# A fused attention and feed-forward kernel: first loads made plain, the first chunk's mask put on TensorE, x transposed by DMA, feed-forward in smaller pieces, and a planner with priorities

## The chip, the cores and the metric

The kernel runs on one core of one Trainium2 chip. The metric is device time in microseconds (us) of one execution; lower is better. For the kernel before there are three timed runs and one profiled execution. A busy time or a duration below is from that profiled execution, whose times count from the first instruction.

## The reference

Block-sparse attention, and then a feed-forward layer on its output. Four batches, 8 heads, 768 positions, head size 64. The mask works on blocks of 32 positions: neighbours, the first and the last block, and three sampled blocks for each block of queries.

```python
scores = q @ k.T / sqrt(64)
mask = |block_i - block_j| <= 1, or block 0 / 23 on either side, or block_j in sampled_blocks[block_i]
attn = softmax(where(mask, scores, -1e9))
x = (attn @ v) as 3072 tokens x 512            # 4*768 tokens, 8 heads * 64
xn = x / sqrt(mean(x*x) + 1e-6) * rms_g
g = xn @ w_gate                                # 512 x 1536
val = xn @ w_val                               # 512 x 1536
out = (g * sigmoid(g) * val) @ w_out           # 1536 x 512, float32
```

## The kernel before

Work is cut into 12 chunks of 256 queries, three to a batch. A chunk has 12 tiles: 4 pairs of heads (`pr`) by 3 pairs of key blocks (`j2`). For a tile, `scores` (L448) runs four matmuls of 256 columns into a two-bank PSUM tile `s_` (two buffers, token `s`). Each contracts over 64 rows, the two heads of a pair sitting in rows 0 to 63 and 64 to 127. `exp_` (L459, ACT) turns `s_` into the bf16 tile `pt`, `mask_` (L466, DVE) multiplies `pt` by the 0/1 tile `Mk`, and `av` (L479) multiplies it with `va`, which carries a column of ones, into `o_` (one buffer, token `o`). After a pair's three tiles `o_norm` (L491, L494, DVE) divides by the sum of the row and writes `x`. After four pairs `square` (L502, ACT) and `rstd` (L508, L510, POOL) give the RMS factor, `scale_x` (L515, DVE) applies it, `x_transposes` (L525, PE) turns the chunk over into PSUM, and `x_copy` (L532, DVE) writes `xn`, scaled by `gcol`.

The feed-forward of chunk u has six steps f. In each, `product` (L608) makes 8 matmuls for the gate (`gp`) and 8 for the value (`vp`), in one of three one-bank buffers (token `f`). ACT takes tanh (`th`, L618), DVE makes `uu` (L622) and `hp` (L632). `ff_y` (L642) then makes two halves of 12 matmuls of 512 columns; ACT copies each out (`yo`, L649), and the SP queue stores it (L651).

The opening loads batch 0 by casting DMAs on the POOL queue (`load_q` L198, `load_k` L202, `vraw` L258), transposes q and k on PE (`tq`, L328) with copies on DVE and ACT (L334), and builds the masks with GpSimd selects (`Bm`, `Kind`), matmuls (`qm` L367, `mp` L375) and copies (L389, L381). Weights come by four half loads and `wo` (L299, L302). Later batches are loaded piece by piece (L208, L412) and q and k are transposed by DMA on the SP queue (L355).

The order of nearly all this is set by `Plan`, which runs when the kernel is built. Each task has engines with assumed durations, dependencies and tokens. At each step the task with the least key is put on its engine: the start time, then a priority. A gate adds `HOLD` to the time of a scores task that would run too far ahead of the feed-forward (`LEAD` tiles), or whose pair of `s` buffers isn't both free soon. `SOLO` says up to which tile scores tasks hold one tile; from there on they hold two. With `SOLO = 144` all of the 144 tiles are single tasks, and two of them stand side by side only where the planner happens to put them so. Engines then run their lists strictly in that order.

Of the kernel before, what the change touches and what calls it, by code (L numbers as in the profile page):

```python
# [15 lines left out]
HOLD = 1.0  # L16


class Plan:
# [10 lines left out]
    def add(self, name, engines, fn, deps=(), prio=5, acq=(), rel=(), mode=None, lat=0.12,  # L30
            dma=None, after=0.0, gate=None, work=0.0):
        self.seq += 1
        assert name not in self.tasks, name
        self.tasks[name] = dict(
            name=name, engines=engines, fn=fn, deps=list(deps), prio=prio, acq=list(acq),
            rel=list(rel), mode=mode, lat=lat, dma=dma, after=after, gate=gate, work=work,
            seq=self.seq)
# [5 lines left out]
    def run(self, log=None):  # L43
        self.free = free = {e: 0.0 for e in ("PE", "ACT", "DVE", "POOL", "SP")}
        busy = {e: 0.0 for e in free}
# [3 lines left out]
        dma_free = 17.0  # L49
# [15 lines left out]
        while left:  # L65
            best = None
            for name in ready:
# [17 lines left out]
                for e, dur in t["engines"].items():  # L85
# [4 lines left out]
                    key = (round(eager + wait, 3), t["prio"], start + dur, t["seq"])  # L90
# [36 lines left out]
def kernel(  # L127
# [32 lines left out]
    ppool = ctx.enter_context(tc.tile_pool(name="ppool", bufs=3))  # L160
# [14 lines left out]

    plan = Plan()
    for name, n in (("s", 2), ("o", 1), ("f", 3), ("pt", 3), ("x1", 2), ("x2", 3), ("xn", 3),
                    ("hp", 2), ("th", 3), ("uu", 3), ("yo", 3), ("qk", 2), ("raw", 1)):
        plan.pool(name, n)

    samp_i = const.tile([32, 2 * NRND], I32, name="samp_i")
# [4 lines left out]
    gcol = const.tile([P, KC], FP32, name="gcol")  # L186
    nc.sync.dma_start(out=gcol, in_=moe_rms_g.rearrange("(c p) -> p c", p=P))
# [16 lines left out]
    def load_c(b, i, c):  # L204
# [7 lines left out]
    load_q(0, 2, 0, 2)  # L212
    load_k(0, 2)

# [4 lines left out]
    nhalf = const.tile([P, 2], FP32, name="nhalf")  # L219
    nc.vector.memset(nhalf, -0.5)  # L220
    Bm = const.tile([32, 32], BF16, name="Bm")
    nc.vector.memset(Bm, 1.0)
    Kind = const.tile([32, NC, P], BF16, name="Kind")
    nc.vector.memset(Kind, 1.0)
    Kindf = Kind.rearrange("b c p -> b (c p)")
# [3 lines left out]
    jb = const.tile([32, 32], I32, name="jb")  # L229
    nc.gpsimd.iota(jb, pattern=[[1, 32]], base=0, channel_multiplier=0)  # L230
    nc.gpsimd.affine_select(
        out=Bm, in_=Bm, compare_op=ALU.is_ge, fill=0.0,
        base=1, pattern=[[-1, 32]], channel_multiplier=1)
    nc.gpsimd.affine_select(
        out=Bm, in_=Bm, compare_op=ALU.is_ge, fill=0.0,
        base=1, pattern=[[1, 32]], channel_multiplier=-1)
    for base in (0, -(NB - 1)):
        nc.gpsimd.affine_select(
            out=Bm, in_=Bm, compare_op=ALU.not_equal, fill=1.0,
            base=base, pattern=[[0, 32]], channel_multiplier=1)  # L240
    nc.gpsimd.affine_select(
        out=Kind, in_=Kind, compare_op=ALU.is_ge, fill=0.0,
        base=0, pattern=[[1, NC], [NC, P]], channel_multiplier=-32)
    nc.gpsimd.affine_select(
        out=Kind, in_=Kind, compare_op=ALU.is_ge, fill=0.0,
        base=31, pattern=[[-1, NC], [-NC, P]], channel_multiplier=32)

# [3 lines left out]

    load_q(2, 8, 0, 2)
    load_k(2, 4)
    load_k(4, 8)
    va = [const.tile([P, H, NC, D + 2], BF16, name=f"va{i}") for i in range(2)]
    vraw = raw.tile([P, H, NC * D], BF16, name="vraw")
    for lo in (0, 4):
        nc.gpsimd.dma_start(out=vraw[:, lo:lo + 4, :], in_=vv[0, :, lo:lo + 4, :])  # L258
# [8 lines left out]
    jbf = const.tile([32, 32], FP32, name="jbf")  # L267
# [3 lines left out]
    nc.vector.memset(Bm[:, 0:1], 1.0)  # L271
    nc.vector.memset(Bm[:, NB - 1:NB], 1.0)
    for r in range(NRND):
        nc.vector.scalar_tensor_tensor(
            out=Bm[0:NB, 0:NB], in0=jbf[0:NB, 0:NB], scalar=samp_f[0:NB, r:r + 1],
            in1=Bm[0:NB, 0:NB], op0=ALU.is_equal, op1=ALU.max)

# [9 lines left out]
    def pe(cols, n=1):  # L287
# [3 lines left out]
    K_AT = {0: 5.5, 1: 9.0, 2: 12.0, 3: 12.0}  # L291
    V_AT = (15.0, 17.6)
    plan.add("qrest", {"POOL": 0.8}, lambda e: load_q(0, 8, 2, 6), deps=[">wg0", ">wv0"], dma=4.2,
             prio=5, after=9.0)
    for half in range(2):
        for nm, dst, src in (("wg", wg, wgv), ("wv", wv, wvv)):
# [42 lines left out]
    for pr, i, c0, c1 in TP:  # L339
# [4 lines left out]
                 deps=["qrest"] if c0 else [])  # L344
# [15 lines left out]
    Qvis = const.tile([32, S], BF16, name="Qvis")  # L360
    Mk = const.tile([P, NIC, NC, CQ], BF16, name="Mk")
    mps = {}

    def mask_query(ic):
        cols = slice(ic * CQ, (ic + 1) * CQ)
        qm = fbank("qm")
        nc.tensor.matmul(  # L367
            out=qm[0:32, 0:CQ], lhsT=Bm[0:NB, :], rhs=Kindf[0:NB, cols], start=True, stop=True)
        mps["q", ic] = qm

    def mask_tile(ic, j2):
        mp = fbank("mp")
        cols = slice(ic * CQ, (ic + 1) * CQ)
        for j in range(2):
            nc.tensor.matmul(  # L375
                out=mp[:, j * CQ:(j + 1) * CQ], lhsT=Kind[0:NB, 2 * j2 + j, :],
                rhs=Qvis[0:NB, cols], start=True, stop=True)
        mps[ic, j2] = mp

    def mask_copy(e, ic, j2):  # L380
        (nc.scalar.copy if e == "ACT" else nc.vector.tensor_copy)(  # L381
            out=Mk[:, ic, 2 * j2:2 * j2 + 2, :].rearrange("p j q -> p (j q)"),
            in_=mps.pop((ic, j2)))

    for ic in range(NIC):
        at = 8.0 if ic == 0 else 14.0 + 4 * ic
        plan.add(f"mq{ic}", {"PE": 0.3}, lambda e, ic=ic: mask_query(ic), acq=["f"], mode="m",
                 prio=1 + ic, after=at, lat=0.2)
        plan.add(f"mqc{ic}", {"DVE": dve1(256)}, lambda e, ic=ic: nc.vector.tensor_copy(  # L389
            out=Qvis[:, ic * CQ:(ic + 1) * CQ], in_=mps.pop(("q", ic))[0:32, 0:CQ]),  # L390
            deps=[f"mq{ic}"], rel=["f"], prio=0)
        for j2 in range(NC // 2):
            plan.add(f"mt{ic}_{j2}", {"PE": 0.3}, lambda e, ic=ic, j2=j2: mask_tile(ic, j2),
                     deps=[f"mqc{ic}"], acq=["f"], mode="m", prio=1 + ic, lat=0.2)
            plan.add(f"mk{ic}_{j2}", {"DVE": dve1(512), "ACT": act(512)},
                     lambda e, ic=ic, j2=j2: mask_copy(e, ic, j2),
                     deps=[f"mt{ic}_{j2}"], rel=["f"], prio=0)
# [3 lines left out]
    for b in range(1, B):  # L401
# [9 lines left out]
        for c in range(NC):  # L411
            plan.add(f"v{b}_{c}", {"POOL": 0.9}, lambda e, b=b, c=c: nc.gpsimd.dma_start(  # L412
# [15 lines left out]

    st, pts, ots, x1s, x2s, mss = {}, {}, {}, {}, {}, {}
# [5 lines left out]
    LEAD = 28  # L435
    SPEED = 1.0
    SOLO = 144
# [3 lines left out]
    def scores(t):  # L441
# [4 lines left out]
        for jj in range(2):  # L446
            for e in range(2):
                nc.tensor.matmul(  # L448
                    out=s_[:, e, jj * CQ:(jj + 1) * CQ],
                    lhsT=x[64 * e:64 * e + 64, 1, 2 * j2 + jj, pr, :],  # L450
                    rhs=x[64 * e:64 * e + 64, 0, 2 * ic:2 * ic + 2, pr, :],
                    start=True, stop=True)
# [33 lines left out]
    def o_norm(ch, pr):  # L486
# [6 lines left out]
        for qt in range(2):  # L493
            nc.vector.tensor_tensor(  # L494
                out=x1s[ch][:, qt, 2 * pr:2 * pr + 2, :], in0=o4[:, qt, :, 0:D],
                in1=rz[:, 2 * qt:2 * qt + 2].unsqueeze(2).to_broadcast([P, 2, D]), op=ALU.mult)
# [32 lines left out]
    def x_copy(ch):  # L529
        xns[ch] = xpool.tile([P, KC, CQ], BF16, name="xn", tag="xn", bufs=3)  # L530
        for c in range(KC):
            nc.vector.tensor_scalar(  # L532
                out=xns[ch][:, c, :], in0=xts[ch][:, c, :],
                scalar1=gcol[:, c:c + 1], scalar2=None, op0=ALU.mult)

    SPT = {}
# [3 lines left out]
    for run in runs:  # L540
# [8 lines left out]
        if prev:  # L549
            deps.add(">" + prev)  # L550
        prev = f"s{i}"
        plan.add(f"s{i}", {"PE": pe(256, 2 * len(run))}, lambda e, run=run: [scores(t) for t in run],
                 deps=sorted(deps), acq=["s"] * len(run), mode="s", prio=2, lat=0.2,
                 gate=lambda i=i: (i % 2 or not PAIRED or plan.soon("s", 2)) and i <= LEAD + SPEED * len(TILES) * plan.done_work / FTOT)
# [5 lines left out]
    for ch, pr, j2 in TILES:  # L560
# [4 lines left out]
        if prev:  # L565
# [3 lines left out]
        plan.add(f"m{n}", {"DVE": dve2(1024)}, lambda e, t=(ch, pr, j2): mask_(t),  # L569
                 deps=[f"x{n}", f"mk{ic}_{j2}"], prio=3)  # L570
        deps = [f"m{n}"]
        if b == 0:
            deps.append(f"va0_{pr // 2}")
        else:
            deps += [f"v{b}_{c}" for c in (2 * j2, 2 * j2 + 1)]
        if j2:
            deps.append(f">av{ch}_{pr}_{j2 - 1}")
        plan.add(f"av{n}", {"PE": 8 * 0.0292}, lambda e, t=(ch, pr, j2): av(t),
                 deps=deps, acq=["o"] if j2 == 0 else [], rel=["pt"] if j2 == NJ - 1 else [],
                 mode="f", prio=3, lat=0.2)  # L580
    for ch in range(NCH):
        for pr in range(NP):
            plan.add(f"on{ch}_{pr}", {"DVE": 0.2 + 2 * dve1(128)},
                     lambda e, ch=ch, pr=pr: o_norm(ch, pr), deps=[f"av{ch}_{pr}_{NJ - 1}"],
                     acq=["x1"] if pr == 0 else [], rel=["o"], prio=1)
# [5 lines left out]
        for qt in range(2):  # L591
            plan.add(f"sc{ch}_{qt}", {"DVE": dve2(512)}, lambda e, ch=ch, qt=qt: scale_x(ch, qt),
                     deps=[f"rs{ch}"] + ([f">sc{ch}_0"] if qt else []), acq=["x2"],
                     rel=["x1"] if qt else [], prio=0)
        plan.add(f"xt{ch}", {"PE": 0.46}, lambda e, ch=ch: x_transposes(ch),
                 deps=[f"sc{ch}_0", f"sc{ch}_1"], acq=["f", "xn"], rel=["x2", "x2"], mode="f", prio=0, lat=0.2)
        plan.add(f"xc{ch}", {"DVE": 4 * dve2(256)}, lambda e, ch=ch: x_copy(ch),
# [5 lines left out]
    def product(w, u, fp, name):  # L603
        pp = fbank(name)
# [31 lines left out]
    YP = 3  # L636
# [90 lines left out]
```

## Time and profile before

| what | value |
|---|---|
| median of 3 runs | 326.82 us (326.37 to 327.65) |
| profiled execution | 325.57 us, its span 323.9 us |
| mean granted TensorE clock | 0.979 |
| busy share of the span | PE 94%, DVE 77%, ACT 66%, POOL 24% |
| first feed-forward matmul | at 37.46 us |
| one chunk where it has settled | 24.26 us |

The profiled execution is 1.25 us under the median of the runs, and its span 1.67 us under its own time. A span that is worked out for the changed kernel therefore becomes a time by adding 1.67 us, and a median by 1.25 us more. A busy PE is not a PE at its peak, since ends of matmuls are modelled; starts are what durations are taken from where instructions follow one another.

### The profile page before, as it was taken

The numbers are of one execution on the slowest core, as the hardware profiler recorded it, in microseconds if no ns is written. First come the engines' busy times: TensorE is split into PE (matmuls) and PEld (weight loads), VectorE is DVE, ScalarE is ACT, GpSimd is POOL, SyncE is SP. The second block draws the span as 40 slices with busy tenths as digits, with TensorE's granted clock in tenths as the row PEclk, the third lists the DMA queues.
The fourth block names the chain that finished last, engine by engine and source line by source line (L and its number), as shares of the span: only waits on it lengthen the run. The fifth ranks groups of instructions, "written<-read, shape, count | busy, mean of one in ns | idle before, by whom it ended". The sixth has DMA issues, their size and how long they took to land.

```text
span 323.9 us, 8037 instructions
## 1 busy us (share of the span) xinstructions
PE 304.8 (94%) x3368; PEld 204.2 (63%) x3389; DVE 249.4 (77%) x533; ACT 214.3 (66%) x296; POOL 76.5 (24%) x107
## 2 busy tenths in 40 slices
PE   6875999997999999999999999999999999999995
PEld 2353677575657756757747757757757757768682
DVE  4596799787958979977977968968968968957280
ACT  1684489879579676676676776776776776643221
POOL 8841747105942119070010010010010010010000
PEclk9995699999999999999999999999999999999999
DMA  3999999973999709999000000000000000010101
GB/s 35 171 210 206 208 167 134 157 151 26 143 153 196 72 2 155 94 148 192 4 32 34 2 32 34 2 32 35 2 34 33 2 34 32 2 35 32 47 21 65
DMA packets 87016, 25.68 MB, mean 79 GB/s; under 512 B 77252, under 2 KB 83908, under 8 KB 86980
## 3 DMA queue, kind: packets, MB, share of 16 engines
q0 software_dynamic: 64048, 14.16, 53.4%
q1 hardware_dynamic: 22932, 11.02, 16.0%
q8 instruction: 26, 0.43, 0.6%
q14 instruction: 10, 0.08, 0.1%
HBM read 28.31 MB, written 6.29 MB: 107 GB/s over the span
## 4 chain that ended last, share of the span: by engine, by line
PE 82%; DVE 9%; ACT 3%; POOL 2%; issue 2%; DMA 1%; POOLq 0%; DVEq 0%; ACTq 0%
PE yp L642 20%; PE gp L608 18%; PE vp L608 18%; DVE pt L466 3%; PE xT L525 1%; PE tq L328 1%; ACT junk L502 1%; DMA kb<-in_k_dram 1%; DVE uu L622 1%; ACT pt L459 1%; DVE hp L632 1%; DVE x L494 1%; PE mp L375 1%; DVE x L515 1%; POOL rs L510 1%
## 5 line engine op out<-in xcount | busy, mean ns | idle before, releaser
L466 DVE TENSOR_TENSOR pt<-pt,Mk 128x1024 bf16<-128x1024 bf16 x144 | 98.5, 698 | 10.1 <-ACT pt L459 8.9
L608 PE MATMUL vp<-xn,wv 128*128 128x256 bf16 x576 | 74.8, 273 | 0.2 <-DVE hp L632 0.2
L608 PE MATMUL gp<-xn,wg 128*128 128x256 bf16 x576 | 74.7, 273 | 0.1
L642 PE MATMUL yp<-wo,hp 128*128 128x512 bf16 x267 | 68.4, 380 | 1.3 <-DVE hp L632 0.2
L618 ACT ACTIVATE th<-gp 128x512 bf16<-128x512 f32 x72 | 43.1, 599 | 34.4 <-PE gp L608 34.4
L608 PEld LDWEIGHTS <-wv 128*128 128x128 bf16 x576 | 53.5, 98 | 11.9 <-issue 4.9
L622 DVE SCALAR_TENSOR_TENSOR uu<-th,gp 128x512 bf16<-128x512 bf16 x72 | 49.1, 683 | 15.0 <-ACT th L618 14.6
L608 PEld LDWEIGHTS <-wg 128*128 128x128 bf16 x576 | 52.5, 98 | 9.2 <-issue 2.3
L479 PEld LDWEIGHTS <-pt 128*128 128x128 bf16 x1152 | 45.8, 99 | 18.4 <-issue 7.8
L632 DVE TENSOR_TENSOR hp<-uu,vp 128x512 bf16<-128x512 bf16 x72 | 49.2, 684 | 6.3 <-PE vp L608 2.6
L508 POOL TENSOR_SCALAR rs<-ms 128x2 f32<-128x2 f32 x12 | 2.8, 233 | 189.4 <-ACT junk L502 189.4
L642 PEld LDWEIGHTS <-hp 128*128 128x128 bf16 x288 | 24.6, 97 | 26.2 <-issue 4.6
L448 PEld LDWEIGHTS <-qkT 64*128 64x128 bf16 x576 | 19.2, 95 | 30.5 <-issue 27.3
L649 ACT ACTIVATE yo<-yp 128x512 f32<-128x512 f32 x24 | 14.3, 596 | 17.4 <-PE yp L642 17.3
L515 DVE TENSOR_SCALAR x<-x,rs 128x512 bf16<-128x512 f32 x24 | 11.9, 536 | 15.6 <-POOL rs L510 15.6
L412 POOL DMA_DIRECT2D va<-in_v_dram x18 | 16.1, 948 | 7.9 <-PE o__2376 L479 7.4
L208 POOL DMA_DIRECT2D qb<-in_q_dram x18 | 15.8, 922 | 6.4 <-DMA wo<-in_moe_w_out_dram 5.6
L208 POOL DMA_DIRECT2D kb<-in_k_dram x18 | 16.3, 924 | 3.0 <-DMA qkT<-kb 3.0
L502 ACT ACTIVATE junk<-x 128x512 bf16<-128x512 f32 x24 | 14.8, 625 | 1.8 <-DVE x L494 1.8
L532 DVE TENSOR_SCALAR xn<-xT,gcol 128x256 bf16<-128x256 bf16 x48 | 13.5, 343 | 1.6 <-PE xT L525 1.5
L525 PE MATMUL xT<-ident,x 128*128 128x128 bf16 x96 | 7.9, 226 | 5.5 <-DVE x L515 3.6
L525 PEld LDWEIGHTS <-x 128*128 128x128 bf16 x96 | 6.4, 100 | 8.2 <-DVE x L515 4.2
(479 smaller groups left out, 364.1 us busy)
## 6 DMA issues: line engine op xcount, KB each, us to landing
out_dram<-yo SPq DMA_DIRECT2D x24, 256.0 KB, 2.0
kb<-in_k_dram POOLq DMA_DIRECT2D x18, 128.0 KB, 5.6
qb<-in_q_dram POOLq DMA_DIRECT2D x18, 128.0 KB, 6.6
va<-in_v_dram POOLq DMA_DIRECT2D x18, 128.0 KB, 7.4
wg<-in_moe_w_gate_dram POOLq DMA_DIRECT2D x2, 768.0 KB, 16.2
wv<-in_moe_w_val_dram POOLq DMA_DIRECT2D x2, 768.0 KB, 19.2
wo<-in_moe_w_out_dram POOLq DMA_DIRECT2D x1, 1536.0 KB, 29.6
vraw<-in_v_dram POOLq DMA_DIRECT2D x2, 384.0 KB, 8.3
```

Of the source, the lines that this page charges most:

```text
L208: nc.gpsimd.dma_start(out=flat[:, c * DM:(c + 1) * DM].rearrange("p (h d) -> p h d", h=H), in_=src[b, :, :, c * D:(c + 1) * D])
L412: plan.add(f"v{b}_{c}", {"POOL": 0.9}, lambda e, b=b, c=c: nc.gpsimd.dma_start(out=va[b % 2][:, :, c, 0:D], in_=vv4[b, :, :, c, :]), deps= ...
L448: nc.tensor.matmul(out=s_[:, e, jj * CQ:(jj + 1) * CQ], lhsT=x[64 * e:64 * e + 64, 1, 2 * j2 + jj, pr, :], rhs=x[64 * e:64 * e + 64, 0, 2 ...
L466: nc.vector.tensor_tensor(out=pv, in0=pv, in1=m.unsqueeze(1).to_broadcast([P, 2, 2 * CQ]), op=ALU.mult)
L479: nc.tensor.matmul(out=o_[:, qt, e, 0:D + 1], lhsT=pt[:, j2, e, jj * CQ + qt * P:jj * CQ + (qt + 1) * P], rhs=va[(ch // NIC) % 2][:, 2 * p ...
L502: nc.scalar.activation(out=junk, in_=x1s[ch][:, qt].rearrange("p h d -> p (h d)"), func=AF.Square, scale=float(DM) ** -0.5, accum_out=mss[ ...
L525: nc.tensor.transpose(out=xts[ch][:, c, qt * P:(qt + 1) * P], in_=x2s[ch, qt][:, c * P:(c + 1) * P], identity=ident)
L608: nc.tensor.matmul(out=pp[:, i * CQ:(i + 1) * CQ], lhsT=w[:, c, f * P:(f + 1) * P], rhs=xns[u][:, c, :], start=(c == 0), stop=(c == KC - 1))
L618: nc.scalar.activation(out=ths[u, fp], in_=gst[u, fp], func=AF.Tanh, scale=0.5)
L622: nc.vector.scalar_tensor_tensor(out=uus[u, fp], in0=ths.pop((u, fp)), scalar=1.0, in1=gst.pop((u, fp)), op0=ALU.add, op1=ALU.mult)
L632: nc.vector.tensor_tensor(out=hps[u][:, 2 * fp:2 * fp + 2, :].rearrange("p f t -> p (f t)"), in0=uus.pop((u, fp)), in1=gst.pop((u, fp, "v" ...
L642: nc.tensor.matmul(out=yst[u, t], lhsT=hps[u][:, f, t * P:(t + 1) * P], rhs=wo[:, f, :], start=(f == 0), stop=(f == NF - 1))
```

## The change

- Constants of the planner: `HOLD` 41.978, `LEAD` 29, the priority (from a table `PRIO`) times `SOFT` is added to the key's time, and engines start at times other than zero.
- `SOLO = 24`: from tile 24 on, scores tasks hold two tiles.
- Opening: the first heads of q and k are loaded plain in float32 by the ACT and SP queues (`qf`, `kf`) and cast on ACT; `v` of batch 0 is loaded plain by SP and cast by POOL. POOL's selects for the mask are replaced by one iota and DVE operations. The rest of q is loaded ahead of the weights.
- Chunk 0 (`PEMASK`) has no `mask_`: each of its scores matmuls is followed by one that adds a large negative number where the mask is 0 (`KindG`, `NegQ`). The `Mk` tiles come later.
- `av` of chunk 0 uses an `f` bank for each second pair; `pt` has four buffers and not three.
- `o_norm` is one operation for the two query halves. `scale_x` multiplies by the RMS factor and `gB` (rms_g broadcast) at once.
- Chunks 1 to 10: x is transposed by two DMAs on the SP queue straight into `xn`. Chunks 0 and 11 keep PE and one copy.
- Feed-forward: each product is cut into two tasks of four matmuls, `ff_y` into six parts, each of which waits only for the `hp` it reads. The last steps use `s` buffers. The last output is copied and stored in two halves.

```diff
-HOLD = 1.0
+HOLD = 41.978
+SOFT = 0.0051
+LEAD = 29
+PRIO = {'av': 4, 'e': 6, 'g': -5, 'h': -6, 'm': 16, 'mk': -2, 'mt': 4, 'on': -2, 'rs': 21, ...}
-                    key = (round(eager + wait, 3), t["prio"], start + dur, t["seq"])
+                    key = (round(eager + wait + SOFT * t["prio"], 3), start + dur, t["seq"])
...
+    nc.sync.dma_start(out=kf, in_=kv[0, :, 0:2, :])
+    nc.scalar.dma_start(out=qf, in_=qv[0, :, 0:2, 0:2 * D])
...
+        nc.gpsimd.memset(vraw[:, lo:lo + 4, 0:1], 0.0)
+        nc.sync.dma_start(out=vraw[:, lo:lo + 4, :], in_=vv[0, :, lo:lo + 4, :])
...
-    SOLO = 144
+    SOLO = 24
...
                 nc.tensor.matmul(
                     out=s_[:, e, jj * CQ:(jj + 1) * CQ],
...
-                    start=True, stop=True)
+                    start=True, stop=ch not in PEMASK)
+                if ch in PEMASK:
+                    nc.tensor.matmul(
+                        out=s_[:, e, jj * CQ:(jj + 1) * CQ], lhsT=KindG[rows, 2 * j2 + jj, :],
+                        rhs=NegQ[rows, ic * CQ:(ic + 1) * CQ], start=False, stop=True)
...
-        nc.vector.tensor_scalar(
+        nc.vector.scalar_tensor_tensor(
             out=x2s[ch, qt], in0=x1s[ch][:, qt].rearrange("p h d -> p (h d)"),
-            scalar1=mss[ch][:, qt:qt + 1], scalar2=None, op0=ALU.mult)
+            scalar=mss[ch][:, qt:qt + 1], in1=gB, op0=ALU.mult, op1=ALU.mult)
...
+    def x_dma(ch, qt):
+        if qt == 0:
+            xns[ch] = xpool.tile([P, KC, CQ], BF16, name="xn", tag="xn", bufs=3)
+        nc.sync.dma_start_transpose(
+            out=xns[ch][:, :, qt * P:(qt + 1) * P], in_=x2s[ch, qt])
+
+    XDMA = range(1, NCH - 1)
...
+                 gate=lambda i=i: (i % 2 or not PAIRED or i < SOLO or plan.soon("s", 2)) and i <= plan.lead + ...)
...
-    YP = 3
+    YP = 6
...
+        if (u, t) == (NCH - 1, 1):
+            lo, hi = slice(0, DM // 2), slice(DM // 2, DM)
```

What the lists look like is seen at three places. The first is ACT's list in the settled part, where an `ACTIVATE pt` is the exp of one scores tile (the number in `s__` names the PSUM tile), `th` the tanh of a feed-forward step. Before:

```order
L459 ACTIVATE pt<-s__4574 128x1024
L618 ACTIVATE th<-gp 128x512
L459 ACTIVATE pt<-s__4609 128x1024
L618 ACTIVATE th<-gp 128x512
L459 ACTIVATE pt<-s__4651 128x1024
L618 ACTIVATE th<-gp 128x512
```

After:

```order
L525 ACTIVATE pt<-s__3785 128x1024
L525 ACTIVATE pt<-s__3790 128x1024
L715 ACTIVATE th<-gp 128x512 x2
L525 ACTIVATE pt<-s__3873 128x1024
L525 ACTIVATE pt<-s__3878 128x1024
L715 ACTIVATE th<-gp 128x512
```

Scores tiles, which had stood one by one between the feed-forward steps, stand in twos. Counted over PE's whole list, the scores matmuls stand in 116 unbroken runs before and in 79 after; from the first gate matmul on, in 108 and in 66. Of tiles 12 to 143, 23 runs of two and 86 of one have become 61 of two and 10 of one.

The second is DVE's list in chunk 0, from the copies of the transposed q and k to the first division. Before:

```order
L334 COPY qkT<-tq 128x6x128
L466 TENSOR_TENSOR pt<-pt,Mk 128x1024 x3
L491 RECIPROCAL rz<-o__313 128x4
L494 TENSOR_TENSOR x_340<-o__313,rz 128x128 x2
L466 TENSOR_TENSOR pt<-pt,Mk 128x1024
L389 CAST Qvis<-qm 32x256
L491 RECIPROCAL rz<-o__358 128x4
```

After:

```order
L298 COPY Bm<-Bm 24x24
L365 COPY qkT<-tq 128x2x128
L365 COPY qkT<-tq 128x6x128
L365 COPY qkT<-tq 128x2x128
L365 COPY qkT<-tq 128x6x128
L365 COPY qkT<-tq 128x2x128 x2
L365 COPY qkT<-tq 128x6x128 x2
L558 RECIPROCAL rz<-o__350 128x4
```

The multiplications by `Mk` have gone from chunk 0, and the whole making of `Bm` now stands on DVE ahead of the first copy of `qkT`.

The third is SP's list, from the first transposes of x on; it had held only stores and the transposes of k and q. After:

```order
L605 DMA_TRANSPOSE xn<-x_1000 128x4x128
L605 DMA_TRANSPOSE xn<-x_1046 128x4x128
L386 DMA_TRANSPOSE qkT<-kb 128x12x128
L754 DMA out_dram<-yo 128x512
L386 DMA_TRANSPOSE qkT<-kb 128x12x128
L386 DMA_TRANSPOSE qkT<-qb 128x8x128
L754 DMA out_dram<-yo 128x512
L605 DMA_TRANSPOSE xn<-x_1282 128x4x128
L605 DMA_TRANSPOSE xn<-x_1293 128x4x128
```

Before, the same stretch was:

```order
L355 DMA_TRANSPOSE qkT<-kb 128x12x128
L651 DMA out_dram<-yo 128x512
L355 DMA_TRANSPOSE qkT<-kb 128x12x128
L651 DMA out_dram<-yo 128x512
L355 DMA_TRANSPOSE qkT<-qb 128x8x128 x3
L651 DMA out_dram<-yo 128x512
```

The two transposes of chunk 2's x (`x_1282`, `x_1293`) come behind two stores and three transposes of batch 1, each of which waits for its own input.

More of the change, by code (lines that the diff above doesn't have):

```diff
@@ L44, in run @@
         self.free = free = {e: 0.0 for e in ("PE", "ACT", "DVE", "POOL", "SP")}
+        free.update(DVE=4.6, POOL=4.5, ACT=1.5)
         busy = {e: 0.0 for e in free}
@@ L218 @@
     nc.vector.memset(ident, 0.0)
[L219 to L225, printed above, removed]
     nc.gpsimd.affine_select(
@@ new lines, in mask_copy @@
+        if e == "ACT":
+            nc.scalar.activation(
+                out=dst, in_=mps.pop((ic, j2)), func=AF.Identity, scale=1.0 / BIG, bias=ones[:, 0:1])
+        else:
+            nc.vector.tensor_scalar(
+                out=dst, in0=mps.pop((ic, j2)), scalar1=1.0 / BIG, scalar2=1.0,
+                op0=ALU.mult, op1=ALU.add)
+    for i in range(2):
+        plan.add(f"kr{i}", {"PE": 0.3}, lambda e, i=i: key_rows(i), acq=["f"], mode="m",
+                 prio=0, after=3.6, lat=0.2)
+        plan.add(f"kc{i}", {"DVE": dve1(384), "ACT": act(384)}, lambda e, i=i: key_copy(e, i),
+                 deps=[f"kr{i}"], rel=["f"], prio=0)
@@ L385 @@
     for ic in range(NIC):
-        at = 8.0 if ic == 0 else 14.0 + 4 * ic
         plan.add(f"mq{ic}", {"PE": 0.3}, lambda e, ic=ic: mask_query(ic), acq=["f"], mode="m",
[L388 to L391, printed above, removed]
+                 prio=0, after=QAT[ic], lat=0.2)
+        plan.add(f"mqc{ic}", {"DVE": dve1(256), "ACT": act(256)}, lambda e, ic=ic: query_copy(e, ic),
+                 deps=[f"mq{ic}"], rel=["f"], prio=0)
@@ L613, in ff_g, with WIDE, product @@
-    def ff_g(u, fp):
-        gst[u, fp] = product(wg, u, fp, "gp")
+    WFROM = 4
+    def WIDE(u, fp):
+        return u == NCH - 1 or u == NCH - 2 and fp >= WFROM
+    wide = {}
+    def product(w, u, fp, name, half):
+        if WIDE(u, fp):
+            if (u, fp) not in wide:
+                wide[u, fp] = ps_s.tile([P, 2, 512], FP32, name="gv", tag="s")
+            pp = wide[u, fp][:, 0 if name == "gp" else 1]
+        elif half == 0:
+            pp = fbank(name)
+        else:
+            pp = gst[u, fp, name]
+        gst[u, fp, name] = pp
+        f = 2 * fp + half
+        for c in range(KC):
+            nc.tensor.matmul(
+                out=pp[:, half * CQ:(half + 1) * CQ], lhsT=w[:, c, f * P:(f + 1) * P],
+                rhs=xns[u][:, c, :], start=(c == 0), stop=(c == KC - 1))
```

282 lines of the change are left out of this document (173 added, 109 removed).

## The prediction

> **What bounds the kernel now.** I read the busy shares first, with the page's slices of PE and of its clock.
>
> ```profile
> PE 304.8 (94%) x3368; PEld 204.2 (63%) x3389; DVE 249.4 (77%) x533; ACT 214.3 (66%) x296; POOL 76.5 (24%) x107
> ...
> PE   6875999997999999999999999999999999999995
> ...
> PEclk9995699999999999999999999999999999999999
> DMA  3999999973999709999000000000000000010101
> ```
>
> Each digit is a slice of 8.1 us. PE is filled from slice 5 on but for slice 9, and in slices 3 and 4 (24 to 40 us) it is half idle at a clock of 0.5 and 0.6. So there are three parts: an opening of about 37 us, a dense stretch with few stalls, and a settled part. Next I read the stages (columns: window, its length, busy time of PE, PEld, DVE, ACT, POOL, then clock, DMA share, GB/s).
>
> ```profile
> 24.00:32.00 8.00, 4.86 (x55) 3.47 (x54) 5.11 (x13) 4.22 (x8) 0.76 (x2) 0.50 1.26 206
> ...
> 64.00:88.00 24.00, 21.39 (x248) 15.72 (x246) 21.30 (x43) 18.82 (x27) 11.87 (x15) 1.00 1.04 107
> ...
> 213.13:237.39 24.26, 24.15 (x272) 15.88 (x272) 19.70 (x43) 17.52 (x25) 0.92 (x2) 1.00 0.06 23
> ```
>
> One settled chunk takes 24.26 us with PE busy for 24.15 and DVE for 19.70: PE's own work is the time there, and DVE has 19% to spare. What that work costs is read from the chain of waits, on which PE's rows follow one another without gaps (start, us, what): first singles, from the settled part, then a pair, from the dense one.
>
> ```profile
> 244.66 0.33 PE s__4172 L448 x4
> ...
> 248.02 0.87 PE gp L608 x8
> 248.89 0.32 PE s__4249 L448 x4
> 249.22 0.98 PE vp L608 x8
> ```
>
> ```profile
> 39.41 0.32 PE s__597 L448 x4
> 39.74 0.22 PE s__602 L448 x4
> ```
>
> Eight product matmuls take 0.87 us, but 0.98 behind a scores tile, and a lone scores tile takes 0.32, while the second of two takes 0.22. So a lone tile costs 0.32 + 0.11 = 0.43, and a pair 0.32 + 0.22 + 0.11 = 0.65: every run of scores carries 0.21 us that isn't streaming, and joining two singles saves that. The opening's chain shows a different limit.
>
> ```profile
> 17.50 3.51 DVE pt L466 x3
> ...
> 23.34 1.20 DVE Mk L381 x2
> 24.54 1.20 DVE pt L466 x2
> 25.74 0.33 DVE Qvis L389
> ...
> 26.12 1.43 PE mp L375 x6
> 27.55 1.62 PE o__460 L479 x24
> ...
> 29.73 1.34 ACT junk L502 x4
> ...
> 31.46 0.74 POOL rs L510
> ...
> 37.53 1.01 PE gp L608 x8
> ```
>
> From 17.5 on it runs over masks, mask tiles and then the one serial way from chunk 0's attention to the first feed-forward step. PE waits there for others.
>
> **The opening.** Two rows of the timeline give the first and the last of chunk 0's 12 exps.
>
> ```profile
> 8.23 1.02 ACT L459 ACTIVATE pt<-s__172 128x1024 bf16<-128x1024 f32 x1 [6.15 <-PE s__172 L448]
> 9.15 1.02 ACT L459 ACTIVATE pt<-s__177 128x1024 bf16<-128x1024 f32 x1
> ...
> 24.70 1.02 ACT L459 ACTIVATE pt<-s__407 128x1024 bf16<-128x1024 f32 x1
> ```
>
> The first two start 0.92 us apart, so 12 need 11.0 us, and they took 17.5 (8.23 to 25.72). The other 6.5 us were waits: for the second and third loads of q and k, and for `o_` and `pt`, held by masks on DVE. The change takes both away. Masks leave DVE for chunk 0; PE gets four more matmuls for each tile, 12 x 0.2 to 0.4 us, beside ACT's 0.92 for each, hence on no path. The second and third loads of k are now issued behind POOL's selects:
>
> ```profile
> 5.31 0.85 POOL L244 TENSOR_SCALAR_AFFINE_SELECT Kind<-Kind 32x768 bf16<-32x768 bf16 x1
> ...
> 6.97 1.49 POOL L202 DMA_DIRECT2D kb<-in_k_dram x2
> ```
>
> They come about 3 us sooner, as only one iota (768 columns, so some 0.85), `ident`, three small iotas and the load of q (0.9) stand ahead.
>
> The first exp is the uncertain one. The plain loads have no row of their kind; the nearest are the store of `yo` and the casting load of k.
>
> ```profile
> out_dram<-yo SPq DMA_DIRECT2D x24, 256.0 KB, 2.0
> ...
> kb<-in_k_dram POOLq DMA_DIRECT2D x1, 384.0 KB, 6.5
> ```
>
> 384 KB of `kf` land 2 to 6.5 us after 0.8. The cast, the transposes (0.85) and DVE's longer list ahead of the first copy then give a first exp between 7 and 11 us. I take 8.5, not sooner than now, because DVE now makes `Bm` first; and since the load is SP's first it lies nearer to the store. With 0.5 us of gaps the last exp ends at 20.0 instead of 25.7.
>
> From there the serial way is priced by these rows and the chain's:
>
> ```profile
> L622 DVE SCALAR_TENSOR_TENSOR uu<-th,gp 128x512 bf16<-128x512 bf16 x72 | 49.1, 683 | 15.0 <-ACT th L618 14.6
> ```
>
> ```profile
> 16.94 0.56 DVE L334 COPY qkT<-tq 128x768 bf16<-128x768 bf16 x1 [0.27 <-PE tq L328]
> ...
> 29.41 0.49 DVE L494 TENSOR_TENSOR x<-o__460,rz 128x128 f32<-128x128 f32 x2
> ```
>
> The last `av` 0.6, division 0.7, two squares 1.34, `rstd` 1.0, two `scale_x` (two sources, as `uu`) with a mask copy between them 3 x 0.68 = 2.0, transposes 0.6, one copy of 1024 columns 0.7, and about 1.2 for the copies and the mask that DVE's list has in between: 8.1 us, where it is now 11.8 (25.7 to 37.5; mask products and a slow `av` go). The first gate step starts at 28.1: **-9.4**. Weights cover that: until then 4.7 MB of batch 0 and 3.1 MB of first halves must be read, and at 206 GB/s written in bf16, twice that read, they are in after some 19 us, at 21 to 23 us. If chunk 0 is bound by data after all, at the 6.5 bound, the gain is about 5.
>
> **Scores in pairs.** From the first gate step on there are 42 fewer runs: 42 x 0.21 = **-8.8**. Nothing hides this, as PE is the bound. It asks for both `s` buffers at once, which singles did not.
>
> **x by DMA.** On PE a chunk's eight transposes take
>
> ```profile
> 241.80 0.45 PE xT L525 x8
> ```
>
> and the copies out of PSUM, on the timeline, 1.12 of DVE,
>
> ```profile
> 242.54 1.12 DVE L532 TENSOR_SCALAR xn<-xT,gcol 128x256 bf16<-128x256 bf16 x4
> ```
>
> so ten chunks give PE **-4.5**. DVE loses those four copies in each chunk, gains about 0.4 in `scale_x` (two sources) and saves 0.4 in `o_norm`: near 18.6 us in a chunk of 22.5, 83% where it is 81%. That pays nothing by itself and bounds nothing. The new way is longer, and what hides it is the work between a chunk's last `av` and its first gate step. By PE's list and the rows above this is 22 us in the settled part, but 11.8 us for chunk 2 (9 product groups of 0.87, 12 `yp` of 0.22 (4.93 over 22, below), two pairs of scores) and 11.6 for chunk 3. In it go division, squares, `rstd`, scaling (0.7 + 1.34 + 1.0 + 1.36 = 4.4), queueing behind DVE (1.5), and the two DMAs. The nearest row to these is the transpose of q, eight blocks of 128 by 128 against four.
>
> ```profile
> qkT<-qb SPq DMA_TRANSPOSE x9, 5.0
> ```
>
> A half is then between 2.5 (in proportion) and 5.0, and both, one behind the other, 5 to 10; I take 6, since a fixed part stands in every transfer. 4.4 + 1.5 + 6 = 11.9 just fits. On the SP queue chunk 2's two stand behind stores and transposes whose inputs come, by the same sum, up to 62 us, and x at about 64. So I add 1.5 us for chunks 2 and 3 and nothing later.
>
> On this the Trainium skill, VectorE: DVE Perf Modes, section "The three transpose paths", speaks against the change: it has 1309 ns for a 128 by 128 block through the DMA crossbar and 390 ns on TensorE, and advises TensorE where PSUM will do. By that figure, as an estimate, two halves would take 10.5 us and the sum would be some 8 us higher; the rows of q and k give 0.62 us a block, and the sum goes by them.
>
> **The rest.** At the first gate step four more scores tiles and one more `av` group lie behind than before (4 x 0.22 + 0.23): **-1.1**. On the other side 15 mask matmuls now come after it, 15 x 0.12 (1.43 for six at half clock) with about four more runs: **+2.6**. Chunk 0's masks were counted. Halved products and `ff_y` in six parts issue the same matmuls; each part of `ff_y` waits for its own `hp` alone, where the last two sums had waited for all, and the last store and its copy are halved.
>
> ```profile
> 314.94 4.93 PE yp L642 x22
> ```
>
> ```profile
> 319.88 0.60 ACT L649 ACTIVATE yo<-yp 128x512 f32<-128x512 f32 x1 [1.99 <-PE yp L642]
> ```
>
> I give both together -0.4, most of it the copy of 0.60. The waits of the dense stretch (2.6 us of idle PE in 64 to 88) stay, since DVE is as full there (21.3 of 24).
>
> **Sum.** 325.57 - 9.4 - 8.8 - 4.5 + 1.5 - 1.1 + 2.6 - 0.4 = 305.5. The profiled execution lies 1.25 under the median, so 306.7.
>
> **The rivals.** *The opening's gain is lost.* The plain `v` load (1.57 MB, twice as many bytes written) runs beside q, k and the weights, `va` is late, and the `av` in PE's list block the scores behind them. Against it stands 206 GB/s in bf16, which is 412 read already. For it: DMA engines are at 9 tenths from 8 to 64 us. It would give 312 to 316, by losing 6 to 9.4.
>
> *x is late through the dense stretch.* If a transpose lands like the worst of its kind, beside batch loads, chunks 2 to 4 wait 3 to 4 us each.
>
> ```profile
> DMA to landing us min/median/max: 3.2/5.3/10.6
> ```
>
> That gives 310 to 317; the settled part keeps 22 us of cover. The page's figure above would make it 314, and the median here speaks against it.
>
> *Pairs wait for ACT.* A pair needs both `s` buffers; if the exp of the tile before isn't done, the second tile holds PE up and all behind it. Two pairs show that.
>
> ```profile
> PE s__943 L448 <- ACT pt L459: 0.5, 1, 0.5
> PE s__1337 L448 <- ACT pt L459: 0.5, 1, 0.5
> ```
>
> With this in each of 61 pairs the cost is 30 us, and the kernel is slower: 327 to 337. It decides from 0.33 us a pair (20 us over 61). Against it: only 2 of 26 pairs had it, ACT is busy for 17.5 of 24.26, and a pair comes each 3.75 us with 1.9 of exps.
>
> **How the numbers follow.** The forecast, with its sizes off by up to 6 either way (299 to 312): 0.64. The opening lost: 0.12. x late: 0.14. Pairs waiting, in some or all: 0.06, of which 0.02 end near no change. Better than all this, below 299: 0.04. The range, 299 to 318, holds the first three. A difference under 0.5% can't be told from none here. Faster 0.94, same 0.02, slower 0.04.
>
> **What would show it.** The first `gp` at 28 (26 to 31); last exp of chunk 0 at 20; a settled chunk of 22.5 us (24.26 less 6 x 0.21 and 0.45) with PE over 98% busy; 79 runs of scores; transposes of x landing in 3 to 4 us; no wait of a gate step for `xn` past chunk 4. It would be wrong if a settled chunk is still 24 us, if PE shows idle time ahead of each second scores tile, or if the first `gp` is at 34 or later.

## The result and the profile after

The changed kernel takes 318.78 us (median; 318.47 to 320.11) against 326.69 in the same session: ratio 0.9761, 95% interval 0.9726 to 0.9795. It is faster, by 8 us where 20 were forecast, and lies just above the range's end of 318. The profiled execution took 320.11 us with a span of 318.3; it was the longest of the four.

The page's busy shares and slices of the changed kernel (a slice is 8.0 us):

```profile
PE 294.2 (92%) x3337; PEld 206.2 (65%) x3359; DVE 229.4 (72%) x439; ACT 213.2 (67%) x300; POOL 70.9 (22%) x102
...
PE   7998991999899999999999999999999999997975
...
PEclk9999997699999999999999999999999999999999
DMA  7999999869999989999921020020020020010101
```

The half-idle, half-clocked slices 3 and 4 of the kernel before (24 to 40 us) are gone. In their place slice 6 (48 to 56 us) has PE at one tenth, with the clock low there and in the next slice, and the last four slices, which were nearly full, have gaps. Stage by stage (window, its length, busy time of PE, PEld, DVE, ACT, POOL, then clock, DMA share, GB/s):

```profile
24.00:32.00 8.00, 6.71 (x94) 4.10 (x89) 7.45 (x14) 8.00 (x13) 5.58 (x8) 1.00 1.16 210
48.00:56.00 8.00, 0.64 (x6) 0.42 (x5) 1.36 (x3) 1.34 (x2) 6.25 (x9) 0.72 2.63 152
56.00:64.00 8.00, 7.74 (x61) 4.50 (x62) 6.19 (x13) 3.85 (x5) 0.00 (x0) 0.64 0.77 98
64.00:88.00 24.00, 22.71 (x235) 17.15 (x238) 18.92 (x32) 15.23 (x23) 6.19 (x8) 1.00 1.15 116
184.38:207.20 22.82, 22.61 (x263) 15.98 (x264) 18.58 (x35) 17.30 (x25) 0.92 (x2) 1.00 0.12 36
```

The opening and the settled chunk came close to the forecast: the first feed-forward step starts at 29.65 us (28.1 foretold, 37.5 before), and a settled chunk takes 22.82 us (22.5 foretold, 24.26 before).

```profile
29.65 1.05 PE L709 MATMUL gp<-xn,wg 128*128 128x256 bf16 x8
```

PE's two largest waits name what was not foreseen (engine, tile and line, releaser: us in all, times, longest):

```profile
PE mp L426 <- DVE uu L719: 7.4, 1, 7.4
PE gv L709 <- ACT th L715: 5.5, 8, 0.7
```

**The first, 48.6 to 56.1 us.** PE waits for DVE's `uu`, but DVE isn't busy. DVE's row at that place (start, length, and in brackets its own idle time and releaser), then POOL's list:

```profile
54.64 0.75 DVE L582 SCALAR_TENSOR_TENSOR x<-x,rs,gB 128x512 bf16<-128x512 f32 x1 [7.94 <-POOL rs L577]
```

```profile
31.80 0.88 POOL L219 DMA_DIRECT2D kb<-in_k_dram  x1 [1.44 <-DMA wg<-in_moe_w_gate_dram]
35.92 0.88 POOL L219 DMA_DIRECT2D qb<-in_q_dram  x1 [3.24 <-PE s__761 L510]
43.26 1.74 POOL L219 DMA_DIRECT2D qb<-in_q_dram  x2 [6.46 <-DMA wo<-in_moe_w_out_dram]
45.43 2.63 POOL L219 DMA_DIRECT2D qb<-in_q_dram  x3 [0.43 <-issue]
48.03 4.40 POOL L471 DMA_DIRECT2D va<-in_v_dram  x5
52.64 0.88 POOL L471 DMA_DIRECT2D va<-in_v_dram  x1 [0.20 <-issue]
53.59 0.22 POOL L575 TENSOR_SCALAR rs<-ms 128x2 f32<-128x2 f32 x1
```

Read from the bottom. Chunk 1's `rstd` starts the moment the last load issue is over, so it waited for the queue and not for its input; ACT had finished the squares at 46.0 (its row ends there):

```profile
45.81 0.21 ACT L569 ACTIVATION_READ_ACCUMULATOR junk<-x 128x1 f32 x1
```

Ahead of `rstd` stand batch 1's eighteen load issues, 0.9 us each, and several wait themselves, one 6.46 us for `wo` to land (issued at 8.78, landed 34.2 us later, at 43.0). DVE's list has `scale_x` ahead of `uu`, so DVE stops, then PE. The kernel before has the same order on POOL, all eighteen issues ahead of chunk 1's `rstd`:

```profile
44.32 0.88 POOL L208 DMA_DIRECT2D qb<-in_q_dram  x1 [5.62 <-DMA wo<-in_moe_w_out_dram]
...
54.05 0.88 POOL L412 DMA_DIRECT2D va<-in_v_dram  x1 [0.47 <-DMA qb<-in_q_dram]
57.24 0.40 POOL L508 TENSOR_SCALAR rs<-ms 128x2 f32<-128x2 f32 x1 [2.30 <-ACT junk L502]
```

There the issues were over at 54.9 and POOL still waited 2.3 us for the squares. The change brought the squares forward by 11 us, but the landing of `wo` by 1 (issue released at 43.26 instead of 44.32).

**The second, the last eight feed-forward steps.** PE's timeline there:

```profile
284.04 0.60 PE L709 MATMUL gv<-xn,wv 128*128 128x256 bf16 x4
285.33 0.60 PE L709 MATMUL gv<-xn,wv 128*128 128x256 bf16 x4 [0.69 <-ACT th L715]
285.76 1.04 PE L709 MATMUL gv<-xn,wg 128*128 128x256 bf16 x8
286.64 0.60 PE L709 MATMUL gv<-xn,wv 128*128 128x256 bf16 x4
287.92 0.60 PE L709 MATMUL gv<-xn,wv 128*128 128x256 bf16 x4 [0.69 <-ACT th L715]
```

A step starts every 2.59 us (285.33 to 287.92), where 16 matmuls take 2 x 0.87 = 1.74: the second half of the value product starts only when tanh has read the gate, which lies in the other half of the same two-bank tile. Eight times 0.85 is 6.8 us; the profile books 5.5 of it as waits, as it counts idle time only from the modelled end of the last matmul.

### The profile page after: what moved, and what is told of

It reads as the page before. It is cut to its first block, busy times and chain, and to the rows that moved or that the text cites. A ratio compares the mean times of both kernels' runs of the same rounds, so it can differ in the third digit from the quotient of the medians.

```text
span 318.3 us, 7937 instructions
## 1 busy us (share of the span) xinstructions
PE 294.2 (92%) x3337; PEld 206.2 (65%) x3359; DVE 229.4 (72%) x439; ACT 213.2 (67%) x300; POOL 70.9 (22%) x102
## 4 chain that ended last, share of the span: by engine, by line
PE 68%; DMA 11%; POOL 7%; DVE 6%; ACT 4%; issue 3%; POOLq 0%; ACTq 0%; DVEq 0%
PE yp L736 17%; PE gp L709 14%; PE vp L709 14%; DMA wo<-in_moe_w_out_dram 11%; PE gv L709 5%; ACT junk L569 2%; POOL va L471 2%; ACT th L715 2%; DVE hp L726 2%; DVE x L582 2%; POOL qb L219 1%; DVE uu L719 1%; DVE pt L532 1%; POOL rs L577 1%; POOL qb L209 1%
## 5 line engine op out<-in xcount | busy, mean ns | idle before, releaser
L532 DVE TENSOR_TENSOR pt<-pt,Mk 128x1024 bf16<-128x1024 bf16 x132 | 87.2, 684 | 6.0 <-ACT pt L525 6.0
L709 PE MATMUL vp<-xn,wv 128*128 128x256 bf16 x512 | 69.8, 275 | 0.0
L709 PE MATMUL gp<-xn,wg 128*128 128x256 bf16 x512 | 66.4, 273 | 1.1 <-DVE hp L726 1.1
L709 PEld LDWEIGHTS <-wg 128*128 128x128 bf16 x576 | 56.1, 98 | 10.3 <-issue 1.7
L715 ACT ACTIVATE th<-gp 128x512 bf16<-128x512 f32 x64 | 38.3, 598 | 28.0 <-PE gp L709 26.2
L719 DVE SCALAR_TENSOR_TENSOR uu<-th,gp 128x512 bf16<-128x512 bf16 x64 | 43.6, 682 | 14.5 <-ACT th L715 14.1
L726 DVE TENSOR_TENSOR hp<-uu,vp 128x512 bf16<-128x512 bf16 x64 | 43.6, 682 | 4.0 <-PE vp L709 1.9
L582 DVE SCALAR_TENSOR_TENSOR x<-x,rs,gB 128x512 bf16<-128x512 f32 x24 | 17.6, 748 | 14.8 <-POOL rs L577 14.7
L719 DVE SCALAR_TENSOR_TENSOR uu<-th,gv 128x512 bf16<-128x512 bf16 x8 | 5.5, 687 | 14.9 <-PE gv L709 14.9
L709 PE MATMUL gv<-xn,wv 128*128 128x256 bf16 x64 | 9.6, 272 | 5.5 <-ACT th L715 5.5
L715 ACT ACTIVATE th<-gv 128x512 bf16<-128x512 f32 x8 | 4.8, 597 | 14.3 <-PE gv L709 14.3
## 6 DMA issues: line engine op xcount, KB each, us to landing
wo<-in_moe_w_out_dram POOLq DMA_DIRECT2D x1, 1536.0 KB, 34.2
```

The source lines that it names most:

```text
L532: nc.vector.tensor_tensor(out=pv, in0=pv, in1=m.unsqueeze(1).to_broadcast([P, 2, 2 * CQ]), op=ALU.mult)
L582: nc.vector.scalar_tensor_tensor(out=x2s[ch, qt], in0=x1s[ch][:, qt].rearrange("p h d -> p (h d)"), scalar=mss[ch][:, qt:qt + 1], in1=gB, ...
L709: nc.tensor.matmul(out=pp[:, half * CQ:(half + 1) * CQ], lhsT=w[:, c, f * P:(f + 1) * P], rhs=xns[u][:, c, :], start=(c == 0), stop=(c == ...
L715: nc.scalar.activation(out=ths[u, fp], in_=gst[u, fp, "gp"], func=AF.Tanh, scale=0.5)
L719: nc.vector.scalar_tensor_tensor(out=uus[u, fp], in0=ths.pop((u, fp)), scalar=1.0, in1=gst.pop((u, fp, "gp")), op0=ALU.add, op1=ALU.mult)
L726: nc.vector.tensor_tensor(out=hps[u][:, 2 * fp:2 * fp + 2, :].rearrange("p f t -> p (f t)"), in0=uus.pop((u, fp)), in1=gst.pop((u, fp, "vp ...
```

## The experiments

Times are medians; a ratio is to the kernel before, in the same session. The kernel before had medians from 326.29 to 327.76 us in the four sessions, so a difference in us between kernels of different sessions can be off by up to 1.5. The two repairs, alone and together, ran in the session of 326.29; x on TensorE, the mask on DVE, single scores and the old kernel with pairs ran in that of 327.76. In kernels with the edit to the planner, lines stand 7 higher.

| kernel | us | ratio, 95% interval |
|---|---|---|
| changed | 318.78 | 0.9761 (0.9726 to 0.9795) |
| `rstd` ahead of nine issues | 310.06 | 0.9493 (0.9446 to 0.9541) |
| `rstd` ahead of six issues | 313.56 | 0.9598 (0.9554 to 0.9641) |
| last steps in f banks | 313.05 | 0.9569 (0.9517 to 0.9622) |
| both repairs (first and third) | 302.56 | 0.9262 (0.9221 to 0.9304) |
| both, x on TensorE | 309.13 | 0.9432 (0.9393 to 0.9472) |
| both, chunk 0's mask on DVE | 307.73 | 0.9391 (0.9352 to 0.9431) |
| both, single scores | 318.05 | 0.9707 (0.9660 to 0.9754) |
| before, with pairs | 320.80 | 0.9785 (0.9744 to 0.9827) |
| before, `rstd` ahead of nine issues | 332.43 | 1.0176 (1.0135 to 1.0217) |

### POOL's queue, in two doses

The planner's choice is kept; only the order in which it writes out the instructions is changed.

```
+LATE = [f"l1_0_{c}" for c in range(3, 6)] + [f"vl1_{c}" for c in range(6)]
-            t["fn"](e)
+            emit.append((name, lambda t=t, e=e: t["fn"](e)))
...
+        late = [x for x in emit if x[0] in LATE]
+        emit = [x for x in emit if x[0] not in LATE]
+        at = [x[0] for x in emit].index("rs1") + 1
+        for _, fn in emit[:at] + late + emit[at:]:
+            fn()
```

> The changed kernel with one edit: on POOL, chunk 1's rstd (two instructions) stands ahead of the last nine of batch 1's eighteen load issues instead of behind them all; every other engine's list is the same, instruction for instruction. Theory A (rstd stands behind load issues that wait for earlier DMAs to land, and DVE's list waits for it): rstd starts at 46 to 47 us instead of 53.6, the 7.4 us of idle PE at 48.6 to 56 shrink to under 1.5, the clock in 48 to 64 us is over 0.95 where it was 0.68, and the time falls by 7 to 10 us, from 318.8 to 309-312. Rival (that stretch is bound by the weights and batch 1 arriving, the queue is only where it shows): chunk 3 or the feed-forward waits for a load instead, and the time falls by under 3 us, to 316 or more.

Measured: 310.06, 8.7 us less than 318.78, as the first theory has it. POOL's list, and the stretch of the stall, in this kernel:

```profile
47.34 0.67 POOL L582 TENSOR_SCALAR rs<-ms 128x2 f32<-128x2 f32 x1 [1.81 <-ACT junk L576]
```

```profile
48.00:64.00 16.00, 14.90 (x175) 10.45 (x175) 13.95 (x27) 10.96 (x15) 8.63 (x11) 1.00 1.80 141
```

`rstd` now waits for its input; PE is busy for 14.90 of 16 us where it was 8.38 (0.64 + 7.74), at a clock of 1.00. The lower dose moves only the six loads of v:

```
+LATE = [f"vl1_{c}" for c in range(6)]
```

> The same edit in a smaller dose: chunk 1's rstd stands ahead of the last six load issues (those of v) only. Theory A: those issues start at 48.0 us, so rstd starts there, 5.5 us sooner than 53.6, PE's idle time falls from 7.4 to about 2, and the time falls by 5 to 7 us, to 312-314. Rival (loads are the bound): under 3 us, to 316 or more.

Measured: 313.56, 5.2 us less, with 2.7 us of idle PE left at the same place and 1.4 at a new one:

```profile
PE mp L433 <- DVE uu L726: 2.7, 1, 2.7
PE gp L716 <- DMA xn<-x: 1.4, 1, 1.4
```

A stall that shrinks with the number of issues ahead of `rstd` is the queue's; the rival, that loads bound the stretch, falls. The new wait of 1.4 us is for chunk 2's transposed x, so late x can hold a gate step in another order.

### The control: the same edit in the kernel before

> The control: the kernel before, with the same edit on POOL (chunk 1's rstd ahead of the last nine of batch 1's load issues; all other engines' lists unchanged). Theory A (in the kernel before, the issues were done at 54.9 us and the squares only at 57.2, so the order cost nothing there, and the stall was made by computing sooner against the same loads): no gain, 326 to 330, and nothing of the 8.7 us that the edit brought in the changed kernel. Rival (the edit helps by moving nine loads later, away from the weights or from a busy stretch, whatever rstd does): 2 us or more faster, under 325.

Measured: 332.43, 6.0 us slower than its 326.45. That is outside both ranges, that of no gain (326 to 330) too, but it is against the rival: moving the loads later is no gain in itself. The squares come at 57.7 there, so the nine issues wait for `rstd`, and the scores of the next batch wait for them:

```profile
57.68 0.40 POOL L515 TENSOR_SCALAR rs<-ms 128x2 f32<-128x2 f32 x1 [10.59 <-ACT junk L509]
```

```profile
PE s__1237 L455 <- DMA qkT<-qb: 4.5, 1, 4.5
```

The order that costs 8.7 us in one kernel is worth 6 us in the other. It fitted the old times, and the planner came out with it again when the times had changed.

### The last steps

```
     def WIDE(u, fp):
-        return u == NCH - 1 or u == NCH - 2 and fp >= WFROM
+        return False
```

> The changed kernel with one edit: the last eight feed-forward steps (chunk 11, and chunk 10 from its fifth on) use two PSUM banks of the f pool, one for the gate and one for the value, as all other steps do, instead of one two-bank tile of the s pool; PE's order is the same. Theory B (the second half of a value product waits until tanh has read the gate half of the same tile): the eight waits of 0.7 to 0.9 us go, the stretch from chunk 11's rstd to the end falls from 44.9 to 38-40 us, and the time falls by 5 to 7 us, to 312-314. Rival (three f banks are short there, so the wait only changes its place): under 2 us either way, 317 to 321.

Measured: 313.05, 5.7 us less (7.0 between the two profiled executions, 320.11 and 313.11). PE's matmuls stand in the same order and run without gaps (PE's timeline):

```profile
282.93 1.04 PE L709 MATMUL gp<-xn,wg 128*128 128x256 bf16 x8
283.80 1.04 PE L709 MATMUL vp<-xn,wv 128*128 128x256 bf16 x8
284.68 1.04 PE L709 MATMUL gp<-xn,wg 128*128 128x256 bf16 x8
```

A step starts every 1.75 us; three f banks were enough.

### Both repairs

> Both edits, rstd ahead of nine load issues and the last steps in f banks. If A and B hold and are independent (one acts at 48 to 64 us, the other after 273), their gains add: 12 to 17 us, to 302-307, where the prediction stood at 306.7. If the rivals hold: over 314.

Measured: 302.56, that is 16.2 us less than the change alone; 8.7 + 5.7 = 14.4 is within the intervals (some 1.5 us each). It beats both kernels, and its profile has neither hole:

```profile
PE 288.1 (96%) x3337; PEld 203.6 (68%) x3359; DVE 229.1 (76%) x439; ACT 212.8 (71%) x300; POOL 71.4 (24%) x102
...
PE   7798998999999999999999999999999999999994
...
PEclk9999999999999999999999999999999999999999
```

The other parts of the change are taken out of this kernel, since the two stalls would shift with each new plan; pairs are also put into the kernel before.

### Pairs, added to the old kernel and taken from the new

```
-    SOLO = 144
+    SOLO = 24
```

> The kernel before with one number changed (SOLO 144 to 24): scores run in pairs from tile 24 on, all else by the old planner. The pairs as priced (0.21 us a run, 60 runs fewer): a settled chunk of 23.0 us where it is 24.26, and 8 to 12 us less in all, 314 to 319 against 326.5. Rival 1 (the dense stretch is bound by DVE, so pairs pay only from about 130 us on, 32 runs): 5 to 7 us less. Rival 2 (pairs wait for ACT): no gain or slower, 326 or more.

> Both repairs (rstd ahead of nine load issues, last steps in f banks), and scores as single tiles throughout (SOLO 24 to 144). It measures the pairs inside the changed kernel, without the two stalls. As priced (42 to 60 runs more at 0.21 us): settled chunk 22.8 to 24.1 us, and 9 to 13 us slower than with pairs (302.6), 311 to 316. Rival (the 0.21 us a run is not a cost of the run but of waits that pairs move elsewhere): under 4 us slower, below 307.

Measured: 320.80 (7.0 less than its 327.76) and 318.05 (15.5 more than 302.56; 14.5 by the two ratios). One settled chunk each: the old kernel with pairs, the repaired one, the repaired one with singles.

```profile
210.30:233.66 23.36, 23.07 (x271) 16.55 (x272) 19.41 (x42) 16.98 (x25) 0.92 (x3) 1.00 0.07 24
```

```profile
194.50:217.32 22.82, 22.61 (x266) 15.99 (x266) 18.57 (x35) 17.30 (x25) 0.93 (x3) 1.00 0.12 36
```

```profile
205.15:229.62 24.47, 23.87 (x263) 15.00 (x265) 19.04 (x35) 17.17 (x25) 1.36 (x3) 1.00 0.11 33
```

PE's work falls by 24.15 - 23.07 = 1.08 us in the old order and by 23.87 - 22.61 = 1.26 in the new one; six runs at 0.21 are 1.26. Idle time makes the rest: pairs leave 0.29 us idle in the old chunk (0.11 before), singles 0.60 in the new one (0.21 with pairs). So the price of a run is right where the kernel has settled, and the rivals by which pairs wait for ACT, gain nothing or gain under 4 us fall. Both expectations missed in size, one under its range and one over it.

In the old kernel the 7.0 us is what the first rival gave, 5 to 7 us, because pairs pay only late. The trace bears that out: chunk 6's `rstd` starts at 165.1 us before and at 164.6 with pairs, chunk 8's at 215.0 and 210.3. In 64 to 88 us PE stays idle for 2.3 us there (24.00 less 21.68), where it was 2.6, so the dense stretch is bound by something other than PE's own work; that it is DVE, as the rival says, isn't shown. In the repaired kernel the gain also starts late (chunk 4's `rstd` at 109.0 with pairs and 109.3 with singles, chunk 6's at 148.6 and 156.6). Counted on PE's timeline, singles make about 51 more runs from the first gate step on, some 10.7 of the 15.5 us by 0.21 each. The planner also places the rest anew when it is given singles or pairs, and what of the difference that makes isn't settled.

### x on TensorE

```
-    XDMA = range(1, NCH - 1)
+    XDMA = ()
```

> Both repairs, and x transposed on TensorE in all twelve chunks (XDMA empty). As predicted (0.45 us of PE for each of ten chunks): settled chunk 23.3 us for 22.8, and 4 to 6 us slower than 302.6. Rival 1 (the DMA way costs what it saves, by late x or a full SP queue): within 1.5 us, 301 to 304, or faster. Rival 2 (three f banks are short when xT needs one too): over 7 us slower.

Measured: 309.13, 6.6 us more (5.6 by the two ratios), at the upper end of the 4 to 6 or just over it.

```profile
199.70:223.16 23.46, 23.22 (x274) 16.36 (x273) 19.28 (x36) 17.30 (x25) 0.93 (x3) 1.00 0.07 24
```

A settled chunk has 0.61 us more of PE's work and is 0.64 longer, so ten such chunks would make 6.4. One wait that fits a shortage of f banks shows, in the dense stretch (x's transposes wait 1.0 us for `uu`, which reads a bank); in the settled part there is none, so the second rival has little of it. The transposes in the changed kernel landed sooner than those of q (5.0 before), and no row of PE's waits in it names `xn` (min, median, max):

```profile
DMA to landing us min/median/max: 2.4/3.3/7.7
```

### Chunk 0's mask on DVE

```
-    PEMASK = (0,)
+    PEMASK = ()
-                         deps=[f"rawq{b}"] + ([">" + prev] if prev else []), dma=2.05, prio=20 + b)
+                         deps=[f"rawq{b}"] + ([">" + prev] if prev else [">rs0"]), dma=2.05, prio=20 + b)
```

> Both repairs, and chunk 0's mask multiplied in by DVE as in all other chunks instead of added on TensorE (PEMASK empty; batch 1's loads are kept behind chunk 0's rstd as they were). If the mask on DVE held the opening, as the prediction has it (waits for pt and o_ behind masks): the last exp of chunk 0 ends 2 to 4 us later than 21, the first feed-forward step starts at 31 to 34 us instead of 28.8, and the time rises by 2 to 5 us to 305-308. Rival (the opening is bound by the exps and by v's landing): the first step within 1 us of 28.8 and the time within 1.5 us of 302.6.

Measured: 307.73, 5.2 us more (4.2 by the two ratios). The time is in the expected range, but not by the way that was named. The planner put the whole of chunk 1's attention ahead of the first feed-forward step, which starts at 43.37 us and not at 31 to 34:

```profile
43.37 1.03 PE L716 MATMUL gp<-xn,wg 128*128 128x256 bf16 x8
```

Chunk 0's last exp ends at 22.88, 1.7 us later than with the mask on TensorE (21.18 in the repaired kernel), a little short of the 2 to 4 expected. Chunk 0's `rstd` comes at 38.0, and batch 1's loads, which the second line of the edit keeps behind it, start at 39.3. That masks on DVE hold the opening fits the later exp, but isn't shown by it; how much of the 5.2 us is theirs and how much the other order's isn't told apart.

## Why the prediction was right and wrong

**The step that failed** is the sentence "The waits of the dense stretch (2.6 us of idle PE in 64 to 88) stay", with `rstd` priced at 1.0 us wherever it comes up, as if nothing stood ahead of it on POOL. It looked at DVE alone and took for granted that what lay off the path would stay off it; for a wait ahead of chunk 1's `rstd`, which came at 48.6 to 56.1 us and cost 8.7, the sum has no term. Moving compute by 8 to 11 us against loads that moved by 1 turned POOL's in-order list into the longest wait of the kernel. The profile of before had both numbers: issues over at 54.9, squares at 57.2, so 2.3 us of slack against an opening shortened by 9.4. The price, 8.7 us, is what moving `rstd` alone gave back; of it some 2.8 us, by an estimate from the window's row, are not the wait but the clock after it (7.74 us of work at 0.64). These 2.8 and the 7.4 of idle are more than 8.7; 0.4 of idle was left, and the remaining 1.1 is within the intervals. On such gaps the Trainium skill, TensorE: Matmul & The Clock Gate, section Part 1, says that an idle window of about 3.4 us brings half the clock. The trace agrees as far as its means show: 0.72 and 0.64 in the two stretches around 7.4 us of idle, 1.00 where the gap was gone.

The sentences that 2.6 us of idle stay, and that 1.5 come for late x, were wrong the other way. With both repairs, 64 to 88 us has 0.05 of idle PE, with DVE busy for 19.07 there instead of 21.30, and no wait of PE for x:

```profile
64.00:88.00 24.00, 23.95 (x245) 16.89 (x245) 19.07 (x31) 18.02 (x24) 13.04 (x16) 1.00 1.38 142
```

**The end** is the second step that failed. It was booked as -0.4, for smaller pieces and a halved store. That the last eight steps share a two-bank tile between gate and value had no term at all; removing it gave 5.7 us. Nor did the halved store bring much, since DVE's half waits for ACT's (in the changed kernel ACT's copy starts at 314.47 and takes 0.38; from there to the end it is 3.8 us, where it was 4.0):

```profile
314.88 0.42 DVE L748 TENSOR_SCALAR yo<-yp 128x256 f32<-128x256 f32 x1 [4.12 <-ACT yo L747]
```

**The opening**, -9.4, was -7.8. The first exp came at 9.04 (8.5 said), but the last of chunk 0 ended at 21.99, not 20.0; v's second half was late, as one of the rivals feared, but its cast waited for it 2.3 us and not 6:

```profile
19.06 1.47 POOL L339 CAST va<-vraw 128x1536 bf16<-128x1536 f32 x1 [2.31 <-DMA vraw<-in_v_dram]
```

**Pairs** were priced right by the run (1.26 us of PE's work in a chunk, measured 1.08 and 1.26). The term as a whole, -8.8 for 42 runs wherever they stand, was not: pairs gave 7.0 us in the old order and 15.5 in the repaired one, and next to nothing in the first hundred us of either. The rival of pairs that wait for ACT, the one on the other side, did not come: after the first feed-forward step no such wait is among PE's rows.

**x by DMA**, -4.5, was too small: 6.6. The term took the transposes' own 0.45, where a settled chunk had 0.61 more of PE's work; what the other 0.16 is, perhaps the switch to them and back, no run separates. The Trainium skill, VectorE: DVE Perf Modes, section "Rules for kernel authors", advises TensorE where PSUM will do. Here TensorE is the bound, and its way cost 6.6 us. A half of four blocks landed after 3.3 us, 0.83 us a block with everything in it. The Trainium skill, VectorE: DVE Perf Modes, section "The three transpose paths", has 1309 ns for such a block.

**The sum.** The repaired kernel, 302.56, stands 4.1 us under the forecast of 306.7. The two costs that did not come (2.6 + 1.5) are of that size, but the first step was also 0.7 late (28.83) and the settled chunk 0.3 us longer than 22.5 while x gave more than its term. That these cancel is arithmetic; no run shows it.

## What to carry to other kernels

When a change makes one stream of work earlier, list for every in-order queue what stands ahead of the next small instruction that everybody needs, with the time when each of those is released; slack of 2 us is gone once work moves by 8. Load issues that themselves wait for older loads are bad neighbours of such an instruction, and its right place depends on which of the two comes first: the same edit gave 8.7 us here and cost 6 there. Two products that are read by different engines belong in tiles of their own if the second is still being written while the first is read.

## What the runs showed of the hardware

- An issue on POOL takes 0.9 us and can be held until an older DMA has landed (6.46 us for `wo`), with all of POOL's later work behind it.
- After 7.4 us without matmuls the granted clock was 0.64 over the next 8 us; with 0.4 us at that place it stayed at 1.00.
- A DMA transpose of 128x512 bf16 between two SBUF tiles landed after 3.3 us (2.4 to 7.7), where 2.5 to 5.0 had been taken from q's rows; in the changed kernel PE never waited for it, in another order (the lower dose) once, for 1.4 us.
